# Three early weight conversions placed in later steps of an attention pipeline

## The chip, the cores and the metric

The kernel runs on one core of one Trainium2 chip. The metric is the device time of one execution in microseconds (us). Three executions of the kernel before took 723.31, 723.62 and 725.47 us; the median is 723.62 us.

## The reference

Causal attention with a decay bias, then two feed-forward stages, all in float32. Cut to what matters:

```python
scores = scale * q @ k.T                          # 4 batches, 8 heads, 576 positions, head size 64
cum = cumsum(max(s, 0))
scores = where(causal, -1e9, scores + minimum(-(cum[:, None] - cum[None, :]), 0))
x = softmax(scores) @ v                           # heads joined: 2304 tokens x 512
h = ((x @ w1) * (x @ w2)) @ w3 @ w_out            # w1, w2: 512 x 1024
e = h2 * softmax(h2), h2 = h @ w_in; out = layernorm(e) * g_ln @ w_out2
```

The weights arrive as float64, so the kernel has to turn their bits into float32 itself.

## The kernel before

Attention walks over 32 heads in 36 steps (the loop at line 555). Step `st` computes the scores and the softmax numerators of one head and transposes the probabilities of the head two steps earlier. The first eight heads (batch 0) take steps 0 to 7. Steps 8 and 9 have no scores: they only transpose heads 6 and 7 and multiply by V. From step 10 on, heads 8 to 31 run with the product units of the first feed-forward layer (`ab_unit`, matmuls at line 312, from the table `NF`) between them. The first eight heads use plain float32 matmuls (line 178); later heads use a split into a high and a low word (lines 186 and 187), and each of those splits is made by ACT (line 167, recorded as L94), a DMA (line 168) and one subtraction on POOL (line 169, recorded as L99 on POOL). POOL's first two subtractions, for heads 8 and 9, stand in the steps of heads 6 and 7.

What one head costs on each engine. PE: scores (L178), 13 transposes (L256), and after every second head a pass over V (`av`, L284). DVE: five pieces of row maximum and masking, read from PSUM (L195), a reciprocal (L227, L228), part of the normalisation (L237), and three of six evictions of transposes (L96). ACT: five exponentials (L199), two normalisations (L235), the other three evictions (L94).

A weight conversion (`w_in_job`'s and `wab_job`'s helper `to_f32` at line 345, then `split_w`) takes a staged block of 128 x 512 float64 words and writes a high word and a low word. It is six instructions: ACT scales (L349), DVE shifts (L355) and joins twice (L356, L360), ACT copies the high word (L94, W<-stage), DVE subtracts for the low word (L99, W<-stage,W). All DVE operands lie in SBUF. The block comes by a DMA of 512 KB (L394) into one of two staging buffers; the next load into a buffer waits for the L99 that read it last.

`pump(n)` at line 402 emits n conversions. Its table `PUMP` says how many each step emits, behind the first maximum and exponential of the step's head (`behind`). Sixteen blocks belong to the first layer; three of them are converted before step 10, whose first units need them.

```python
    PUMP = {3: 1, 5: 1, 6: 1, 10: 2, 11: 2, 12: 2, 13: 2, 14: 2, 15: 2, 16: 1}
...
        if st > 1:
            pump(PUMP.get(st, 0))
```

The program's text is not the order on the engines: a scheduler with a model of its own orders each engine's instructions, and the engines then run in that order and wait on semaphores. So a moved conversion can land well away from the step that names it.

Of the kernel before, what the change touches and what calls it, by code (L numbers as in the profile page):

```python
# [26 lines left out]
def tile_attention_moe(  # L27
# [374 lines left out]
    def pump(n):  # L402
        for _ in range(n):
            load_jobs()
            if loaded:
                raw, conv = loaded.pop(0)

                with ExitStack() as order:
                    for ins in behind:
                        order.enter_context(tc.issue_after(ins))  # L410
                    conv(raw)
        load_jobs()
# [135 lines left out]
    steps += [(h if h < NH else None, h - 2 if h >= H + 2 else None) for h in range(H, NH + 2)]  # L548
    NF = {10: 3, 11: 0, 12: 3, 13: 0, 14: 3, 15: 2, 16: 2, 17: 0, 18: 1, 19: 1, 20: 1, 21: 2, 22: 2, 23: 2, 24: 2, 25: 2, 26: 2, 27: 2, 28: 2, 29: 2, 30: 2, 31: 2, 32: 2, 33: 2, 34: 3, 35: 3}
    PD, FS = 10, 0.5  # L550
    PUMP = {3: 1, 5: 1, 6: 1, 10: 2, 11: 2, 12: 2, 13: 2, 14: 2, 15: 2, 16: 1}
    PUMP.update((i, 1 if i < 30 else 2) for i in range(22, 34))
    fill = []
    late = []
    for st, (h, ph) in enumerate(steps):
# [18 lines left out]
        if st > 1:  # L574
            pump(PUMP.get(st, 0))
        if h is not None:
# [461 lines left out]
```

## Time and profile before

| | |
|---|---|
| median of three executions | 723.62 us |
| the profiled execution, its own time | 724.28 us |
| its span, first to last instruction | 722.2 us |
| busy share of PE, DVE, ACT, POOL | 98%, 71%, 65%, 13% |
| mean granted clock of TensorE | 0.998 |
| chain that ended last, by engine | PE 76%, DVE 12%, DMA 4%, ACT 4% |

The profiled execution took 0.66 us more than the median. Its span is 2.1 us shorter than its time; the rest lies before the first and after the last instruction. A busy share over the whole span says little about the first 60 us, where the shares differ from stretch to stretch. "Idle before, releaser" in a row of the timeline is how long the engine stood still ahead of that row and what ended it.

### The profile page before, as it was taken

The page shows a single profiled execution, that of the slowest core. Times are in us where ns is not written, and L with a number is a line of the kernel's source. Part 1 is how long each engine was busy: PE and PEld are TensorE (multiplying, and loading weights), DVE is VectorE, ACT ScalarE, POOL GpSimd, SP SyncE. Part 2 cuts the span into 40 slices and gives each one's busy share as a digit, 9 for nine tenths or more (in the row PEclk, how much of TensorE's full clock was granted, in tenths as well). Part 3 has the DMA queues.
Part 4 walks back from the last instruction along what each step waited for, and adds up shares of the span by engine and source line. Part 5 has one row for each costly group of instructions (what it writes and reads, how often), then busy time and mean ns, then how long its engine had stood idle before and what let it go on. Part 6 is the DMA issues. An engine that isn't in the chain of part 4 may idle for free.

```text
span 722.2 us, 12948 instructions
## 1 busy us (share of the span) xinstructions
PE 706.0 (98%) x4642; PEld 630.9 (87%) x4642; DVE 509.3 (71%) x1252; ACT 467.8 (65%) x978; POOL 94.1 (13%) x88
## 2 busy tenths in 40 slices
PE   9989898999999999999999999999999999999998
PEld 6669888889999999999998889988888988888887
DVE  7997989997878888722787985656747366563751
ACT  7997878798866777822544665656647465564742
POOL 2051322143221221000000000001000000000000
PEclk9999999999999999999999999999999999999999
DMA  4654645454476665514565964242334142303211
GB/s 118 191 138 123 175 154 162 154 147 123 138 231 187 193 183 178 183 63 150 181 209 171 331 207 113 66 110 68 82 87 103 44 131 74 89 13 76 59 45 44
DMA packets 79972, 95.53 MB, mean 132 GB/s; under 512 B 41434, under 2 KB 52954, under 8 KB 79908
## 3 DMA queue, kind: packets, MB, share of 16 engines
q1 hardware_dynamic: 79908, 94.71, 45.2%
q8 instruction: 36, 0.59, 0.3%
q14 instruction: 28, 0.23, 0.1%
HBM read 59.04 MB, written 20.17 MB: 110 GB/s over the span
## 4 chain that ended last, share of the span: by engine, by line
PE 76%; DVE 12%; DMA 4%; ACT 4%; issue 2%; POOL 0%; DVEq 0%; ACTq 0%
PE a L312 12%; PE o L854 12%; PE b L312 12%; PE x L720 11%; PE m L637 6%; PE av L284 4%; PE tr L256 4%; PE hX L752 4%; PE hZ L752 3%; DMA turned<-half 3%; DVE P L195 2%; PE sc L186 2%; PE sc L187 2%; ACT P L199 1%; DMA stage<-in_w_dram 1%
## 5 line engine op out<-in xcount | busy, mean ns | idle before, releaser
L199 ACT ACTIVATE P<-P,STAT 128x576 f32<-128x576 f32 (+4 forms) x160 | 88.2, 553 | 18.7 <-DVE STAT L195 18.1
L99 POOL TENSOR_TENSOR QK<-qk,QK 64x1152 fp32r<-64x1152 f32 x24 | 66.6, 2776 | 169.4 <-ACT QK L94 169.3
L720 PE MATMUL x<-gh,ML 128*128 128x256 f32 x288 | 80.3, 279 | 0.0
L720 PE MATMUL x<-gl,MH 128*128 128x256 f32 x288 | 80.1, 279 | 0.0
L720 PE MATMUL x<-gh,MH 128*128 128x256 f32 x288 | 80.0, 279 | 0.0
L312 PE MATMUL a<-xT0h,W 128*128 128x288 f32 x256 | 58.6, 303 | 3.6 <-ACT PT L94 3.3
L312 PE MATMUL b<-xT0h,W 128*128 128x288 f32 x256 | 57.5, 298 | 1.9 <-DVE g_sb L332 1.7
L854 PE MATMUL o<-OH,lh 128*128 128x512 f32 (+1 forms) x152 | 57.7, 379 | 0.2 <-DVE ll L99 0.2
L816 DVE COPY lt<-turned 128x2048 uint16<-128x2048 uint16 x16 | 21.5, 1344 | 51.1 <-DMA turned<-half 51.1
L854 PE MATMUL o<-OL,lh 128*128 128x512 f32 (+1 forms) x152 | 57.5, 378 | 0.0
L854 PE MATMUL o<-OH,ll 128*128 128x512 f32 (+1 forms) x152 | 57.5, 378 | 0.0
L256 PE MATMUL tr<-ident,P 128*128 128x128 f32 x416 | 54.2, 274 | 3.1 <-DVE PT L96 1.0
L312 PE MATMUL a<-xT1h,W 128*128 128x288 f32 x256 | 57.2, 298 | 0.0
L312 PE MATMUL b<-xT1h,W 128*128 128x288 f32 x256 | 56.5, 294 | 0.0
L720 PEld LDWEIGHTS x<-gl,MH 128*128 128x128 f32 x288 | 54.1, 188 | 1.3
L720 PEld LDWEIGHTS x<-gh,MH 128*128 128x128 f32 x288 | 54.1, 188 | 1.0
L720 PEld LDWEIGHTS x<-gh,ML 128*128 128x128 f32 x288 | 54.1, 188 | 0.8
L96 DVE COPY PT<-tr 64x192 f32<-64x192 f32 (+2 forms) x96 | 40.4, 432 | 17.8 <-PE tr L256 17.8
L349 ACT ACTIVATE stage<-stage 128x512 f32<-128x512 f32 x56 | 37.0, 679 | 24.2 <-DMA stage<-in_w_dram 22.0
L256 PEld LDWEIGHTS tr<-ident,P 128*128 128x128 f32 x416 | 47.1, 141 | 5.8 <-DVE PT L96 1.4
L332 DVE TENSOR_TENSOR g_sb<-b,a_sb 128x288 f32<-128x288 f32 x64 | 28.7, 449 | 30.0 <-PE b L312 20.0
L324 ACT ACTIVATE a_sb<-a 128x288 f32<-128x288 f32 x64 | 25.5, 401 | 36.3 <-PE a L312 36.2
(192 smaller groups left out, 1988.0 us busy)
## 6 DMA issues: line engine op xcount, KB each, us to landing
stage<-in_w_dram SPq DMA_DIRECT2D x32, 512.0 KB
g_scr<-g_sb SPq DMA_DIRECT2D x32, 288.0 KB
stage<-in_wo_dram SPq DMA_DIRECT2D x16, 512.0 KB
qk<-in_qk_dram SPq DMA_DIRECT2D x24, 288.0 KB
QK<-QK SPq DMA_DIRECT2D x24, 288.0 KB
gl<-g_scr SPq DMA_DIRECT2D x24, 256.0 KB
wf<-wf_scr SPq DMA_DIRECT2D x22, 256.0 KB
out_dram<-o SPq DMA_DIRECT2D x17, 256.0 KB
```

Source lines behind the costliest of these rows:

```text
L96: eng.tensor_copy(out=dst, in_=src)
L99: last_lo[0] = eng.tensor_tensor(out=dst, in0=src, in1=hi_.bitcast(F32), op=ALU.subtract).ins
L199: ex = nc.scalar.activation(out=dst, in_=dst, func=AF.Exp, bias=st[0:rows, ti:ti + 1], scale=-1.0, accum_out=st[0:rows, 5 + ti:6 + ti],)
L256: last_tr[0] = nc.tensor.transpose(ps[:, 128 * n:128 * n + 128], pt[:, o:o + 128], ident)
L284: nc.tensor.matmul(st["ps"][64 * e:64 * e + 64, 448 + c0:448 + c1], vr[:, j, e], PT[(2 * p + e) % 4][:, o + c0:o + c1], **kw,)
L312: nc.tensor.matmul(ps, w_[:, c, fs], x_[:, c, sl], start=(c == 0 and w_ is WH and x_ is XH), stop=(c == KC - 1 and w_ is WL),)
L332: ab_last[1] = nc.vector.tensor_tensor(out=g[:, sl], in0=ps, in1=st["a"], op=ALU.mult).ins
L349: nc.scalar.activation(out=high.bitcast(F32), in_=high.bitcast(F32), func=AF.Copy, scale=2.0 ** -112)
L637: nc.tensor.matmul(ps, w_[:, k % 4], o_[:, k], start=(k == 0 and w_ is H3 and o_ is WOH), stop=(k == KF - 1 and w_ is L3),)
L720: last = nc.tensor.matmul(ps[:, a], w_[:, k, m * 128:m * 128 + 128], g_[:, k % 2], start=(k == 0 and w_ is MH and g_ is GH), stop=(k == KF ...
L752: last_h[0] = nc.tensor.matmul(ps, x_[:, k], w_[:, k], start=first and k == 0 and x_ is XH and w_ is WH, stop=k == 1 and x_ is XL, skip_gr ...
L854: last = nc.tensor.matmul(ps, l_[:, k], w_[:, k, c0:c1], start=(k == 0 and l_ is LH and w_ is OH), stop=(k == KF - 1 and l_ is LL),)
```

## The change

One table entry per conversion moves: the first early conversion from step 3 to step 6, the second from step 5 to step 8, the third from step 6 to step 9.

```diff
-    PUMP = {3: 1, 5: 1, 6: 1, 10: 2, 11: 2, 12: 2, 13: 2, 14: 2, 15: 2, 16: 1}
+    PUMP = {6: 1, 8: 1, 9: 1, 10: 2, 11: 2, 12: 2, 13: 2, 14: 2, 15: 2, 16: 1}
```

What the scheduler makes of it, at three places. In the rows, P and STAT_116 to STAT_119 belong to heads whose number leaves 0 to 3 when divided by 4, and PT_112 to PT_115 are the transposed probabilities of the same heads; here they are heads 4 to 7. W_122 and W_123 are the high and low words of w1, W_124 and W_125 those of w2. QK_657 and QK_641 are one tile, that of head 9, under two numbers.

DVE around the last maxima of head 7 (STAT_119), before:

```order
L237 TENSOR_SCALAR P<-P,STAT_118 128x192
L96 COPY PT_112<-tr 64x3x64
L237 TENSOR_SCALAR P<-P,STAT_118 64x64
L195 ISA P,STAT_119<-sc,wmask 128x448
L195 ISA STAT_119 128x1
L195 ISA P,STAT_119<-sc,wmask 64x64
L195 ISA STAT_119 64x1
L99 TENSOR_TENSOR W_123<-stage,W_122 128x4x128
L195 ISA P,STAT_119<-sc,wmask 128x320
L195 ISA STAT_119 128x1
L195 ISA P,STAT_119<-sc,wmask 128x192
L195 ISA STAT_119 128x1
```

and with the change, from the end of the same maxima on:

```order
L99 TENSOR_TENSOR W_125<-stage,W_124 128x4x128
L195 ISA P,STAT_119<-sc,wmask 128x320
L195 ISA STAT_119 128x1
L195 ISA P,STAT_119<-sc,wmask 128x192
L195 ISA STAT_119 128x1
L96 COPY PT_113<-tr 128x512
L237 TENSOR_SCALAR P<-P,STAT_118 64x64
L355 TENSOR_SCALAR stage<-stage 128x512
L96 COPY PT_113<-tr 64x3x64
L96 COPY PT_113<-tr 128x128
L96 COPY PT_114<-tr 128x512
L356 SCALAR_TENSOR_TENSOR stage<-stage 128x512
```

Before, all three conversions end ahead of head 7's last maximum, two of them far ahead. With the change two whole conversions stand between head 6's first maximum and head 7's last one, and the third conversion's L355 and L356 stand among the evictions that follow.

ACT between head 7's exponentials, with the change (before, there is no conversion from the row of QK_657 to the end of head 7's normalisation):

```order
L199 ACTIVATE P,STAT_119<-P,STAT_119 128x448
L199 ACTIVATE P,STAT_119<-P,STAT_119 64x64
L235 ACTIVATE P<-P,STAT_118 128x576
L235 ACTIVATE P<-P,STAT_118 128x448
L94 ACTIVATE QK_641<-qk_587 64x2x576
L94 ACTIVATE PT_113<-tr 128x384
L349 ACTIVATE stage<-stage 128x512
L94 ACTIVATE PT_113<-tr 128x256
L199 ACTIVATE P,STAT_119<-P,STAT_119 128x320
L199 ACTIVATE P,STAT_119<-P,STAT_119 128x192
```

The third conversion's L349 now stands ahead of head 7's last two exponentials; its high word (L94, W_122) stands ahead of head 7's L235, a few rows further on.

SP's queue with the change, where the loads of the third, fourth and fifth block now stand (before, the third and fourth stood ahead of head 8's rows of cum_scr, and the fifth where the third stands now):

```order
L140 DMA qk_743<-in_qk_dram 64x1152
L394 DMA stage<-in_w_dram 128x1024
L158 DMA QK_641<-cum_scr 2x576
L159 DMA QK_641<-cum_scr 2x576
L394 DMA stage<-in_w_dram 128x1024
L168 DMA QK_641<-QK_641 64x2x576
L140 DMA qk_897<-in_qk_dram 64x1152
L394 DMA stage<-in_w_dram 128x1024
L148 DMA VT_120<-in_vm_dram 128x512
```

The loads moved behind the conversions that free their buffers. POOL's order is unchanged throughout, and from the first scores of head 8 on (QK_596 before, QK_580 now) every engine's order is the same as before.

## Rows read from the trace of the kernel before

**Rows 1.** Busy time of one stretch: us, then busy us and count of PE, PEld, DVE, ACT, POOL; PEclk, DMA, GB/s.

```profile
46.00:52.00 6.00, 3.86 (x26) 2.68 (x25) 5.43 (x18) 5.95 (x17) 3.56 (x5) 1.00 0.49 144
```

**Rows 2.** Timeline of PE: start us, us, engine, line, operation, tile, count, idle before.

```profile
35.48 0.44 PE L256 MATMUL tr<-ident,P 128*128 128x128 f32 x2
35.75 1.14 PE L178 MATMUL sc<-QKN 128*128 128x288 f32 x4
...
45.68 1.13 PE L178 MATMUL sc<-QKN 128*128 128x320 f32 x4 [0.27 <-DVE PT L96]
47.78 1.97 PE L256 MATMUL tr<-ident,P 128*128 128x128 f32 x13 [0.97 <-DVE STAT L195]
...
51.69 1.21 PE L256 MATMUL tr<-ident,P 128*128 128x128 f32 x9 [0.79 <-DVE PT L96]
...
57.51 0.47 PE L186 MATMUL sc<-QK 128*128 128x448 f32 x1
```

**Rows 3.** Timeline of DVE from head 6's first maximum to head 7's last one.

```profile
37.58 0.74 DVE L195 CUSTOM_DVE_ANT_0 P<-sc,lmask 128x576 f32<-128x576 f32 x1
...
38.25 0.42 DVE L355 TENSOR_SCALAR stage<-stage 128x512 uint32<-128x512 uint32 x1
...
40.47 0.68 DVE L96 COPY PT<-tr 128x512 f32<-128x512 f32 x1
41.07 0.71 DVE L356 SCALAR_TENSOR_TENSOR stage<-stage 128x512 uint32<-128x512 uint32 x1
...
42.43 2.42 DVE L360 SCALAR_TENSOR_TENSOR stage<-stage 128x512 uint32<-128x512 uint32 x1
44.75 0.60 DVE L237 TENSOR_SCALAR P<-P,STAT 128x320 f32<-128x320 f32 x2
...
45.35 0.28 DVE L96 COPY PT<-tr 128x128 f32<-128x128 f32 x1
...
46.45 0.34 DVE L96 COPY PT<-tr 64x192 f32<-64x192 f32 x1
46.72 0.24 DVE L237 TENSOR_SCALAR P<-P,STAT 64x64 f32<-64x64 f32 x1
...
47.56 0.68 DVE L99 TENSOR_TENSOR W<-stage,W 128x512 fp32r<-128x512 f32 x1
...
48.85 0.75 DVE L99 TENSOR_TENSOR xT0l<-av,xT0h 128x576 fp32r<-128x576 f32 x1
```

**Rows 4.** Timeline of POOL: three of the 24 subtractions of the query and key split.

```profile
41.57 2.71 POOL L99 TENSOR_TENSOR QK<-qk,QK 64x1152 fp32r<-64x1152 f32 x1
...
93.52 3.91 POOL L99 TENSOR_TENSOR QK<-qk,QK 64x1152 fp32r<-64x1152 f32 x1 [10.30 <-ACT QK L94]
109.13 2.68 POOL L99 TENSOR_TENSOR QK<-qk,QK 64x1152 fp32r<-64x1152 f32 x1 [11.69 <-ACT QK L94]
```

**Rows 5.** Timeline of DVE beside the last two of those.

```profile
94.22 0.68 DVE L99 TENSOR_TENSOR W<-stage,W 128x512 fp32r<-128x512 f32 x1
...
109.64 2.46 DVE L355 TENSOR_SCALAR stage<-stage 128x512 uint32<-128x512 uint32 x1
```

**Rows 6.** Timeline of ACT in the step of head 7.

```profile
45.53 0.65 ACT L94 ACTIVATE W<-stage 128x512 fp32r<-128x512 f32 x1
...
46.88 1.33 ACT L235 ACTIVATE P<-P,STAT 128x576 f32<-128x576 f32 x2
...
48.27 0.66 ACT L199 ACTIVATE P<-P,STAT 128x448 f32<-128x448 f32 x1
...
49.38 1.16 ACT L94 ACTIVATE QK<-qk 64x1152 fp32r<-64x1152 f32 x1
```

**Rows 7.** The chain of waits: start us, us, what; the wait for a staged block.

```profile
69.05 3.49 DMA stage<-in_w_dram
```

**Rows 8.** PE's longest wait of the first 200 us, and the stretch behind it (columns as in rows 1).

```profile
119.26 0.58 PE L312 MATMUL a<-xT0h,W 128*128 128x288 f32 x1 [3.34 <-ACT PT L94]
...
120.00:122.00 2.00, 2.00 (x10) 2.00 (x9) 2.00 (x8) 0.87 (x2) 0.00 (x0) 0.50 0.42 149
```

## The prediction

> **What bounds the kernel now.** I read the timeline first, because the change ends where head 8 begins: from its first scores on, every engine's order is unchanged, so whatever it gains or loses is the shift of that one PE row, at 57.51 us [rows 2]. Past it nothing waits on a clock of its own; a shift there is carried to the end one for one.
>
> The busy table by stretch comes next: from 46 to 52 us PE is busy only 3.86 of 6.00 us [rows 1]. In its timeline no row between 24 and 45 us names a wait, and then three long ones do: 0.27, 0.97 and 0.79 us, all of them ended by DVE [rows 2]. From 51.69 us to head 8's scores PE runs unbroken for 5.82 us (9 transposes, a pass over V, 13 transposes). So up to 45 us PE is the limit and conversions lie beside it; from 45 to 52 us DVE is. No row of DVE between 32 and 50 us names a wait.
>
> The last view is DVE against POOL. L360 takes 2.42 us at 42.43, while POOL's subtraction runs from 41.57 to 44.28; its successor starts at 44.75 [rows 3, 4]. L356 just ahead needs 0.71. Unhindered, successors start 0.07 to 0.08 us before a row ends, so L360 costs 0.60 and was held for 1.72.
>
> **The change, part by part.** It removes and adds no work; it moves three conversions.
>
> *Taken out of the time before 36 us.* Up to there DVE sheds all eight rows of the first two conversions and ACT all four of theirs. I cost this at nothing: PE is without a wait, and covers them. What remains is a small gain at head 6's first maximum. DVE reached it at 37.58, after PE had finished the scores of the row at 35.75 [rows 2, 3]. Now DVE is there in time and PE sets it. In the new order the two transposes of 35.48 stand behind those scores, so they take from 35.48 to about 36.5, and DVE starts at 36.6: 0.98 us earlier.
>
> *Put in, up to head 7's last maximum.* Before, that stretch of DVE takes 48.85 - 37.58 = 11.27 us with one conversion in it [rows 3]. The new order has two: 0.34 (L355) + 0.63 (L356) + 0.60 (L360) + 0.61 (L99) = 2.18 us more. It also gains the low word of xT0 (0.67) and one 128 x 128 eviction (0.20) and loses two 64-wide normalisations (0.16 each): +0.55. The hold by POOL's first subtraction stays at 1.72, since some conversion row is there whenever it starts. The stretch is 14.0 us and ends at 36.6 + 14.0 = 50.6, against 48.85. **Term A: +1.75.**
>
> *From there to PE's nine transposes.* Before: 51.69 - 48.85 = 2.84. After: eviction of 512 (0.60), L237 (0.16), the third L355 (0.34), evictions of 64 x 192 and 128 (0.27 + 0.20) [rows 3], and 0.1 to PE: 1.67. **Term B: -1.17.** A and B alone put head 8's scores at 58.1.
>
> *The second hold.* POOL's next subtraction (head 9) starts when ACT has its high words. Behind head 7's second maximum ACT has two exponentials (1.11, the spacing to the next row), L235 (1.23 of the 1.33), and the high words (1.16): 3.5 us [rows 6]. DVE, from the same maximum, has 0.09 + 0.67 + 0.20 + 0.53 + 0.61 + 0.40 + 0.28 + 0.60 + 0.16 = 3.54 us to the third L355 (spans of rows 3 less their overlap; 0.09, 0.40 and 0.28 are the spacings of the reciprocal and the last two maxima). That is a tie. If POOL is first, L355 waits out nearly all of 2.65 us, and the evictions that PE needs wait behind it: +2.6. If DVE is first, the evictions pass (they read PSUM) and L356 is held; head 7's normalisation then sets the end. From POOL's start: 2.65 + L356 0.63 + eviction 0.27 + L360 0.60 + ACT's high word 0.57 [rows 6] + L235 1.23 + 13 transposes 1.57 + 0.2 for hand-overs = 7.7. POOL starts at 50.6 + 1.1 = 51.7, so scores at 59.4, which is 1.3 over 58.1. I take the middle, **term C: +2.0**, as nothing in the rows breaks the tie; the ends are 0 (no conversion row meets it) and 2.6.
>
> That POOL holds L355 so long is a row: 2.46 us at 109.64, beside the subtraction of 109.13 [rows 4, 5]. The other order of arrival is one too: at 93.52 POOL took 3.91 us for what is else 2.7, while DVE's L99 at 94.22 kept its 0.68 [rows 4, 5].
>
> [...]
>
> *DMA.* SP's loads move behind the conversions that free the buffers. The first L99 now ends at about 47.1 (50.6 less the 3.5 us of rows behind it), so the third block lands 3.49 us later [rows 7], at 50.6; ACT reaches its L349 at about 51.7. Slack 1.1 us: no cost. Without it head 7's last two exponentials would stand behind a DMA. SP's own rows of head 9 and 10 now stand behind loads that wait for DVE; their scores start only after 68 us, so I cost that at nothing. V's load behind the fifth block serves heads 8 and 9, equally late.
>
> Sum: 1.75 - 1.17 + 2.0 = **+2.6 us**. The profiled 724.28 would become 726.9; it stood 0.66 above the median of 723.62, so I predict **726.2 us**.
>
> **Rivals.**
>
> *Only the first hold bites (A and B alone).* +0.6 us: 724.2. It needs POOL's second subtraction to run while DVE is in evictions or maxima, as in the step of head 6 where maxima passed beside it. Against it: two SBUF rows of the third conversion stand in just that place.
>
> *Faster: DVE is relieved.* ACT and DVE shed twelve rows before 36 us; if that carries over, DVE meets head 7's maxima early and PE's waits at 45.68, 47.78 and 51.69 vanish, 2.03 us in all: 721.6. If only the holds miss DVE, A falls to 0 and the change gives 1.1: 722.5. It decides if head 7's last maximum ends before 48 us. Against it: PE covers all that is shed, and two conversions come back into the stretch where DVE has no gap.
>
> [...]
>
> *The change doesn't do what it says.* Partly so: by name two conversions move to steps without scores, but on DVE and ACT their rows stand ahead of head 7's last maxima and exponentials. That is in the sum already.
>
> **How the numbers follow.** About 0.3%, 2.2 us, is what a measurement here can tell from no change. Forecast (+1.2 to +3.7): 0.50, of which 0.36 lie above 2.2 us. Worse: 0.12. Only the first hold (0 to +1.2): 0.26. Faster: 0.12, of which 0.08 is by more than 2.2 us, as several waits must vanish at once. So faster 0.08, same 0.14 + 0.26 + 0.04 = 0.44, slower 0.48. The range goes from 722.5, which takes in both holds missing DVE, to 728.2, just short of the clock case in full; somewhat over 0.1 is left out.
>
> **What would show it.** Right: head 7's last maximum ends near 50.6 us in the timeline of DVE; one of the conversion rows between 41 and 46 us takes over 2 us, and L355 or L356 between 51 and 55 us as well; head 8's scores start near 60 us; PE's waits from 45 us on grow from 2 to over 4 us; the span grows as much as that row shifts. Wrong: head 7's last maximum before 49 us, or conversion rows all at their usual 0.4 to 0.7, or head 8's scores late and the span not.

## The result, and the profile after

| | before | after |
|---|---|---|
| median, lowest and highest of 6 runs each (us) | 724.06 (723.04 to 725.47) | 730.65 (728.69 to 732.63) |
| ratio, 95% interval | | 1.0091 (1.0075 to 1.0108) |
| profiled execution, its span (us) | 724.28, 722.2 | 728.69, 726.8 |
| mean granted clock | 0.998 | 0.993 |
| forecast of the median (range) | | 726.2 (722.5 to 728.2) |

The change costs 0.9%. The sign was forecast, the size was not: the median lies 2.45 us above the range. The profiled execution of the changed kernel is the fastest of its six. Of all executions below, one is left out of its ratio: 992.7 us in third_only, at a mean granted clock of 0.656.

The rows below are PE's in the timeline of the changed kernel (columns as in [rows 2]).

```profile
46.78 1.13 PE L178 MATMUL sc<-QKN 128*128 128x320 f32 x4 [1.38 <-ACT PT L94]
...
51.77 1.69 PE L256 MATMUL tr<-ident,P 128*128 128x128 f32 x7 [1.98 <-DVE STAT L195]
55.38 2.18 PE L256 MATMUL tr<-ident,P 128*128 128x128 f32 x9 [1.91 <-DVE PT L96]
57.48 3.79 PE L284 MATMUL av<-PT,VT 128*64 128x64 f32 x24
61.21 1.64 PE L256 MATMUL tr<-ident,P 128*128 128x128 f32 x13
62.80 0.44 PE L186 MATMUL sc<-QK 128*128 128x448 f32 x1
...
124.53 0.58 PE L312 MATMUL a<-xT0h,W 128*128 128x288 f32 x1 [3.34 <-ACT PT L94]
```

Head 8's first scores moved from 57.51 [rows 2] to 62.80, by 5.29 us. The row that stood at 119.26 [rows 8] stands at 124.53, 5.27 later, with the same stop ahead of it. The spans differ by 4.6: some 0.7 comes back after 128 us, 0.31 of it at one wait of PE that shrinks from 0.53 to 0.22 us (at 142.82 before, at 147.73 after). So the place is right: everything is lost before head 8. Two more things are in these rows. The stops of [rows 2] (0.27, 0.97, 0.79) have become 1.38, 1.98 and 1.91, and the first of them is now ended by ACT. And the nine transposes take 2.18 instead of 1.21 us.

The busy table of the same stretch (columns as in [rows 1]) tells why:

```profile
50.00:52.00 2.00, 0.23 (x2) 0.23 (x3) 2.00 (x7) 1.95 (x4) 0.48 (x2) 1.00 0.19 70
52.00:54.00 2.00, 1.41 (x7) 0.77 (x5) 2.00 (x2) 1.98 (x6) 2.00 (x1) 0.61 0.92 314
54.00:56.00 2.00, 0.62 (x3) 0.63 (x4) 2.00 (x6) 0.51 (x3) 0.47 (x1) 0.50 0.54 123
56.00:58.00 2.00, 2.00 (x12) 1.66 (x12) 0.93 (x3) 0.84 (x3) 0.00 (x0) 0.50 0.37 120
58.00:60.00 2.00, 2.00 (x8) 0.94 (x6) 1.96 (x7) 1.68 (x4) 0.00 (x0) 0.68 0.00 0
```

The granted clock falls from 1.00 to 0.50 and stays there until about 59 us. Before, it was 1.00 through this whole stretch:

```profile
52.00:54.00 2.00, 2.00 (x17) 1.44 (x16) 1.87 (x4) 1.56 (x6) 1.25 (x1) 1.00 0.65 134
54.00:56.00 2.00, 2.00 (x20) 1.64 (x16) 0.76 (x4) 1.30 (x4) 0.00 (x0) 1.00 0.57 147
56.00:58.00 2.00, 2.00 (x17) 1.75 (x15) 1.52 (x3) 1.20 (x3) 0.00 (x0) 1.00 0.56 152
```

With the change DVE has no gap from 50 to 56 us, and these are its rows that matter:

```profile
36.74 0.76 DVE L195 CUSTOM_DVE_ANT_0 P<-sc,lmask 128x576 f32<-128x576 f32 x1 [0.92 <-PE sc L178]
...
40.85 0.73 DVE L355 TENSOR_SCALAR stage<-stage 128x512 uint32<-128x512 uint32 x1
41.47 0.67 DVE L237 TENSOR_SCALAR P<-P,STAT 64x64 f32<-64x64 f32 x1
...
44.05 2.10 DVE L356 SCALAR_TENSOR_TENSOR stage<-stage 128x512 uint32<-128x512 uint32 x1 [0.38 <-ACT stage L349]
...
49.23 1.21 DVE L237 TENSOR_SCALAR P<-P,STAT 128x320 f32<-128x320 f32 x2
...
51.64 0.68 DVE L96 COPY PT<-tr 128x512 f32<-128x512 f32 x1
52.25 2.27 DVE L237 TENSOR_SCALAR P<-P,STAT 64x64 f32<-64x64 f32 x1
```

Beside them, POOL (columns as in [rows 4]):

```profile
42.80 2.79 POOL L99 TENSOR_TENSOR QK<-qk,QK 64x1152 fp32r<-64x1152 f32 x1
48.02 0.58 POOL L483 MEMSET QK<- 64x576 f32 x1 [2.43 <-issue]
...
49.68 0.64 POOL L486 MEMSET QK<- 2x576 f32 x1
51.84 2.63 POOL L99 TENSOR_TENSOR QK<-qk,QK 64x1152 fp32r<-64x1152 f32 x1 [1.52 <-ACT QK L94]
```

The two 2 us rows of DVE, L356 and the 64 x 64 L237, lie under POOL's two subtractions; usual are 0.7 and 0.24 us [rows 3]. The pair of L237 at 49.23 lies under the last two of four memsets and takes 1.21 instead of 0.60. The chain of waits carries the first two as pieces of their own:

```profile
44.05 2.10 DVE stage L356
52.32 2.20 DVE P L237
```

### The profile page after: what moved, and what is told of

The parts are those of the page before. It is cut to its first block, busy times and chain, and to the rows that moved or that the text cites. A ratio compares the mean times of both kernels' runs of the same rounds, so it can differ in the third digit from the quotient of the medians.

```text
span 726.8 us, 12951 instructions
## 1 busy us (share of the span) xinstructions
PE 707.8 (97%) x4642; PEld 631.9 (87%) x4642; DVE 510.7 (70%) x1252; ACT 469.1 (65%) x978; POOL 94.4 (13%) x88
## 4 chain that ended last, share of the span: by engine, by line
PE 79%; DVE 10%; DMA 5%; ACT 3%; issue 2%; POOL 0%; DVEq 0%; ACTq 0%
PE a L312 13%; PE b L312 12%; PE o L854 12%; PE x L720 11%; PE m L637 6%; PE av L284 5%; PE tr L256 5%; PE hX L752 4%; PE hZ L752 3%; DMA turned<-half 3%; PE sc L178 2%; PE sc L187 2%; PE sc L186 2%; DVE P L195 2%; PE hW L752 1%
## 5 line engine op out<-in xcount | busy, mean ns | idle before, releaser
L256 PE MATMUL tr<-ident,P 128*128 128x128 f32 x416 | 55.7, 279 | 4.8 <-DVE PT L96 2.1
L96 DVE COPY PT<-tr 128x512 f32<-128x512 f32 (+2 forms) x96 | 40.3, 431 | 19.3 <-PE tr L256 18.7
L349 ACT ACTIVATE stage<-stage 128x512 f32<-128x512 f32 x56 | 36.9, 677 | 23.7 <-DMA stage<-in_w_dram 21.2
L195 DVE CUSTOM_DVE_ANT_0 P<-sc,wmask 128x448 f32<-128x448 f32 (+3 forms) x128 | 47.2, 412 | 2.7 <-PE sc L187 1.7
```

What stands on the lines that cost most here:

```text
L96: eng.tensor_copy(out=dst, in_=src)
L195: mx = nc.vector.tensor_tensor_reduce(out=dst, in0=ps_in, in1=msk, scale=-SCALE, scalar=BIG, op0=ALU.add, op1=ALU.min, accum_out=st[0:rows ...
L256: last_tr[0] = nc.tensor.transpose(ps[:, 128 * n:128 * n + 128], pt[:, o:o + 128], ident)
L349: nc.scalar.activation(out=high.bitcast(F32), in_=high.bitcast(F32), func=AF.Copy, scale=2.0 ** -112)
```

## The experiments

The theory after these rows: POOL's rows hold DVE's (a hold is a row of DVE that lasts longer while a row of POOL runs beside it), PE runs dry, and its clock falls. In most runs below each engine's order is fixed, instruction by instruction, to that of the kernel named, and only the edit differs; "waits for" is a real wait on a semaphore. Lines of an edit are rows of an engine's order. Medians are read by their ratio to the kernel before, run on the same chip.

**The changed kernel again** (after_again).

> The changed kernel once more, for a second profile. Holds theory (POOL's rows hold DVE's, PE runs dry, its clock falls): the same rows again, L356 over 2 us near 44 us, the 64 x 64 L237 over 2 us near 52 us, granted clock at 0.5 from about 53 to 59 us, head 8's first scores at 62.8 us or later; time 730.6 us. Where this profile is slower than the first one (728.7 us), the difference should lie in a longer stretch at the lower clock, here or at 120 us. Rival (a disturbance of the one profiled execution): L356 and L237 at their usual 0.6 and 0.2 us and head 8's scores near 58 us.

730.0 us, 1.0085 (1.0065 to 1.0104). The same holds (the second profile has the same rows), and a lower clock for longer: 0.82, 0.50, 0.50, 0.50 and 0.97 in the five stretches from 52 to 62 us. One row shows it, the pass over V:

```profile
57.17 4.37 PE L284 MATMUL av<-PT,VT 128*64 128x64 f32 x24
```

From the transposes that waited for head 7's last maximum to head 8's scores it took 63.07 - 51.40 = 11.67 us, against 62.80 - 51.77 = 11.03 in the first profile. So these two profiles differ by how long the clock stays down.

**POOL's second subtraction out of the way** (hold2).

```diff
 POOL
-L99 QK<-qk (head 9)
+L99 QK<-qk (head 9), waits for DVE L237 P 64x64 of head 7
```

> Every engine's order is that of the changed kernel; POOL's subtraction for head 9 waits for the last normalisation of head 7 (DVE, near 60 us). Holds theory: the 64 x 64 L237 near 52 us falls from 2.27 to about 0.2 us, head 7's last maximum stays at 51.6 us, head 8's first scores come at 51.6 + 1.7 + 5.8 = 59.1 us, the granted clock stays at 1.00 from 52 to 60 us; the time is 3 to 4 us below the changed kernel's, about 727 us. Work theory (the conversions' own time on DVE is the loss, POOL only stands beside it): head 8's scores stay later than 62 us and the time at 730 us.

726.72 us, 1.0034 (1.0017 to 1.0051): 3.3 us below the changed kernel. DVE first, then PE:

```profile
52.27 0.24 DVE L237 TENSOR_SCALAR P<-P,STAT 64x64 f32<-64x64 f32 x1
```

```profile
51.80 3.74 PE L256 MATMUL tr<-ident,P 128*128 128x128 f32 x16 [1.99 <-DVE STAT L195]
55.47 2.94 PE L284 MATMUL av<-PT,VT 128*64 128x64 f32 x24
...
59.94 0.44 PE L186 MATMUL sc<-QK 128*128 128x448 f32 x1
```

The hold is real, and the scores came 2.86 us earlier. But they missed 59.1: the sixteen transposes took 3.74 us, as the clock fell here too, behind a stop of 1.99 us:

```profile
52.00:54.00 2.00, 2.00 (x10) 1.47 (x10) 1.75 (x6) 1.98 (x6) 0.00 (x0) 0.53 0.80 286
54.00:56.00 2.00, 2.00 (x13) 1.49 (x13) 1.27 (x4) 1.27 (x6) 0.00 (x0) 0.61 0.51 123
```

**PE kept busy in its stops, holds left in place** (fill with 7 unused matmuls of 128 x 512, fill22 with 4).

```diff
 PE
-L284 av 64x64
 L256 tr (head 5), six of nine
+L291 av<-wmask,ident 128x512 x2
 L256 tr x7
+L291 av<-wmask,ident 128x512 x2
 L256 tr x9
+L284 av 64x64
```

They write where the pass over V starts its sums anew; its first 64-wide matmul moves behind the transposes. The trace records each of them as two. The 7 of fill are 3 and 4.

> The order of the changed kernel, with 7 matmuls more on PE that compute nothing used (128 x 512, 3 in the gap before 51.8 us, 4 in the gap before 55.4 us; two 64-wide matmuls of the pass over V are taken from between transposes to its start). Clock theory (the idle PE is what lowered the granted clock, and the lower clock cost 1.6 us): the clock stays near 1.00 from 52 to 60 us, the nine transposes take 1.2 instead of 2.18 us, the pass over V 2.9 instead of 3.8, head 8's scores come at about 61.2 us, and the time is some 1.5 us below the changed kernel's, 729 us, with more work. Rival (the clock falls for another reason, or what PE loses by it is hidden): clock and scores as before, time 730.6 us or up to 1 us more.

> The changed kernel with 4 unused matmuls instead of 7 in PE's two stops (2 and 2), as in the run with 7 those of the second stop ran about 1 us past the eviction that PE waits for. Clock theory: clock at 1.00 or nearly from 52 to 60 us, nine transposes 1.2 us, head 8's scores at 55.4 + 5.8 = 61.2 us or up to 0.5 earlier, time 726 to 727 us, 3 to 4 us below the changed kernel with the same holds in place. Rival (the gain of the run with 7 came from the moved 64-wide matmuls or from elsewhere): no difference to that run, 727.3 us, or a fall of the clock all the same.

fill: 727.31 us (expected: 729), 1.0044 (1.0027 to 1.0061); its clock was 1.00 from 46 to 64 us. fill22: 726.9 us, 1.0020 (1.0003 to 1.0038), with 1.00 from 48 to 62. PE in fill22, and two lines of its busy table:

```profile
52.88 1.88 PE L291 MATMUL av<-wmask,ident 128*128 128x512 f32 x4
55.35 1.20 PE L256 MATMUL tr<-ident,P 128*128 128x128 f32 x9 [0.60 <-DVE PT L96]
...
61.05 0.44 PE L186 MATMUL sc<-QK 128*128 128x448 f32 x1
```

```profile
54.00:56.00 2.00, 1.40 (x8) 0.65 (x7) 2.00 (x6) 0.48 (x3) 0.46 (x1) 1.00 0.68 147
56.00:58.00 2.00, 2.00 (x18) 1.03 (x17) 1.86 (x7) 1.46 (x4) 0.00 (x0) 1.00 0.32 108
```

Nine transposes start when they did (55.38) and take 1.20 instead of 2.18 us; head 8's scores come 1.75 us earlier. More work made the kernel faster, so the lower clock is a price of its own: 1.75 us in the profile, and by the ratios some 3 us (fill) to 5 us (fill22) in the medians, each uncertain by more than 1 us.

**Both edits together** (hold2_fill: hold2, and 2 unused matmuls in the first stop).

> The run with POOL's second subtraction moved, and 2 matmuls more on PE that compute nothing used, in its stop ahead of head 7's last maximum (49.8 to 51.8 us). That run's clock fell to 0.53 and 0.61 from 52 to 56 us although PE was busy from 51.8 us on. Clock theory (that stop alone brings the fall): the clock stays at 1.00 from 52 to 56 us, head 8's scores come 0.8 to 0.9 us earlier (59.1 instead of 59.94 us), the time is about 0.8 us lower or more, 725.5 us. Rival (the fall comes from what PE did after the stop, or from elsewhere): the fall stays, and the time at 726.7 us.

725.73 us, 1.0015 (1.0006 to 1.0024); the clock is 1.00 from 44 to 60 us, and head 8's scores come as expected (59.1):

```profile
59.03 0.44 PE L186 MATMUL sc<-QK 128*128 128x448 f32 x1
```

With that one stop filled, the fall of hold2 is gone.

**POOL's first subtraction out of the way as well** (nohold, then nohold_b).

```diff
 POOL
-L99 QK<-qk (head 8)
 L483 to L486 MEMSET QK (head 9)
+L99 QK<-qk (head 8), waits for DVE L237 P 64x64 of head 6
 L99 QK<-qk (head 9), waits for DVE L237 P 64x64 of head 7
 SP
-L140 qk<-in_qk (head 10)
 L394 stage, L158, L159, L394 stage
+L140 qk<-in_qk (head 10)
 DVE
-L355, L356 (third conversion) among the evictions
+L355, L356 (third conversion) behind them
```

nohold has the waits and the DVE part alone, with POOL's memsets behind its subtraction. "The run before" in its expectation is hold2.

> As the run before, and POOL's subtraction for head 8 and its next four memsets wait for the last normalisation of head 6, with the first two DVE rows of the third conversion behind the evictions that PE waits for. Holds theory: L356 near 44 us takes 0.7 instead of 2.10 us, the two L237 near 49 us 0.6 instead of 1.21; head 7's last maximum ends at about 49.6 us, head 8's first scores come at 49.6 + 1.7 + 5.8 = 57.1 us, as early as in the kernel before (57.5) although both conversions still stand there; time about 724 us. Work theory: head 8's scores at 60 us or later, time 728 us or more.

> As the run in which both subtractions wait, but without what stopped it (ACT stood 7.14 us for the third block, whose load stood on SP behind head 10's words, which waited for POOL): head 10's words are loaded after the two blocks, and POOL makes its second four memsets ahead of the subtraction for head 8. Holds theory: L356 0.7 us, the two L237 near 49 us 1.2 us again (memsets beside them), head 7's last maximum at 51.6 - 1.4 = 50.2 us, head 8's scores at 50.2 + 1.7 + 5.8 = 57.7 us; the granted clock falls little or not, since PE's stop ahead of head 7's last maximum shrinks from 2.0 to 0.6 us; time 724 to 725 us, no slower than the kernel before. Work theory: not below the run with the second subtraction alone moved (726.7 us).

nohold: 734.55 us, 1.0154 (1.0121 to 1.0187). Locally DVE did as expected (L356 0.69, the L237 pair 0.60, head 7's last maximum 2.0 us closer to its first one), but ACT stood still:

```profile
58.99 0.65 ACT L349 ACTIVATE stage<-stage 128x512 f32<-128x512 f32 x1 [7.14 <-DMA stage<-in_w_dram]
```

SP's load of head 10's words waits until POOL has read the buffer, and the third block's load is queued behind it. nohold_b moves it: 726.46 us, 1.0029 (1.0016 to 1.0042). Its DVE, POOL and PE rows:

```profile
44.06 0.69 DVE L356 SCALAR_TENSOR_TENSOR stage<-stage 128x512 uint32<-128x512 uint32 x1 [0.37 <-ACT stage L349]
...
47.86 0.60 DVE L237 TENSOR_SCALAR P<-P,STAT 128x320 f32<-128x320 f32 x2
48.38 0.68 DVE L99 TENSOR_TENSOR W<-stage,W 128x512 fp32r<-128x512 f32 x1
...
49.67 0.68 DVE L96 COPY PT<-tr 128x512 f32<-128x512 f32 x1
```

```profile
48.16 0.82 POOL L483 MEMSET QK<- 64x576 f32 x1 [5.42 <-ACT P L199]
```

```profile
58.83 0.44 PE L186 MATMUL sc<-QK 128*128 128x448 f32 x1
```

Head 7's last maximum now ends at 49.67, 2 us earlier than in the changed kernel, and yet the scores gain only 0.2 us on hold2_fill. PE waits for ACT instead (0.38 us on an eviction, 0.42 on L235), and for a DVE eviction that waited for ACT (0.73). I expected 57.7 and 724 to 725 us, and the time alone is what the work theory said: another bound stood right behind the one taken away.

**ACT's conversion rows behind the evictions, and DVE's behind head 7's normalisation** (nohold_act, then nohold_sp). The two move together; no run parts them.

```diff
 ACT
-L349 stage (third conversion)
 L94 PT x1, L199 x2, L94 PT x4
+L349 stage (third conversion)
-L94 W<-stage
 L235 x2, L94 xT0h
+L94 W<-stage
 DVE
-L355, L356, L360, L99 W (third conversion)
 L227, L96, L228, L237 x3 (head 7)
+L355, L356, L360 (third conversion)
 L96, L99 xT0l, L96
+L99 W (third conversion)
 POOL
-L99 QK<-qk (head 9), waits for DVE L237 P 64x64 of head 7
+L99 QK<-qk (head 9), waits for that L99 W
```

nohold_sp also puts the fifth block's L394 and V's load on SP ahead of head 11's words.

> The run in which neither subtraction meets a conversion, and the third conversion's rows stand behind head 7's: ACT's L349 behind the evictions of head 5 and 6 (it stood ahead of them at 51.44 us), ACT's high word W behind the eviction of the pass over V, DVE's four rows behind head 7's normalisation. There head 8's scores were still at 58.83 us, 1.3 behind the kernel before, with PE waiting 0.73, 0.38 and 0.42 us on evictions and L235. Theory now (holds, and behind them ACT's conversion rows ahead of evictions that PE waits for): those waits shrink to 0.3 us or less, head 8's scores at 57.5 to 57.9 us, as in the kernel before although both conversions stand there; time 724.5 to 725.5 us. Rival (the rest is the DVE work ahead of head 7's last maximum, which isn't touched here): scores stay at 58.8, time at 726.5 us.

> The run with the conversion rows behind head 7's, with one thing more: SP loads the fifth block and V ahead of the words of head 11, which wait for POOL's second subtraction. In that run head 8's scores came at 57.60 us, as in the kernel before, but the block that stood on SP behind those words landed at 69 us, ACT waited 4.56 and DVE 7.00 us for it, and PE stopped for 2.96 and 1.48 us. Theory (POOL's holds and ACT's conversion rows ahead of evictions are the whole loss of the change, and the rest of that run's 730.0 us was the late block): scores at 57.6 us, no stop of PE over 1 us between 62 and 80 us, time 724 to 725.5 us. Rival (two conversions in that stretch cost time in whatever order, later if not there): time at 726.5 us or more with the block there in time.

nohold_act: head 8's scores at 57.60 us, as in the kernel before, but 730.01 us, 1.0076 (1.0056 to 1.0096): a block loaded late stopped PE for 2.96 and 1.48 us near 70 us. nohold_sp: 724.7 us, 1.0011 (0.9991 to 1.0031), with the scores here:

```profile
57.77 0.44 PE L186 MATMUL sc<-QK 128*128 128x448 f32 x1
```

Both conversions still stand ahead of head 7's last maximum, and the time can't be told from that of the kernel before. So their work alone doesn't cost; it cost together with POOL's holds and with the third conversion's rows where the scheduler had put them.

**One part of the change alone** (third_only).

```diff
-    PUMP = {6: 1, 8: 1, 9: 1, 10: 2, 11: 2, 12: 2, 13: 2, 14: 2, 15: 2, 16: 1}
+    PUMP = {3: 1, 5: 1, 9: 1, 10: 2, 11: 2, 12: 2, 13: 2, 14: 2, 15: 2, 16: 1}
```

> One part of the change alone: the first two conversions stay in the steps of heads 3 and 5, only the third moves from head 6's step to the second step without scores. Holds theory: one conversion in the stretch that DVE bounds, as before, and one hold by POOL's first subtraction, now on L355 instead of L360; head 7's last maximum within 0.5 us of 48.85 us, head 8's scores within 1 us of 57.51 us, time 723 to 725 us. Rival (it is the third conversion's move that costs, by its load and its ACT row ahead of head 7's exponentials): most of the loss is there, 727 us or more.

724.98 us, 1.0004 (0.9990 to 1.0018), scores at 57.80 us. One conversion in the stretch costs nothing measurable, in either of the two places tried. Head 7's last maximum ended at 49.78, 0.93 us behind the kernel before and outside the 0.5 that I gave. The hold fell on another row than the L355 that I named, DVE's smallest, of five columns:

```profile
42.73 2.24 DVE L227 TENSOR_SCALAR STAT<-STAT 128x5 f32<-128x5 f32 x1 [0.30 <-ACT P L199]
```

PE had its longest stop of this stretch here, longer than that of hold2, and the clock stayed at 1.00 from 44 to 60 us:

```profile
47.84 1.10 PE L178 MATMUL sc<-QKN 128*128 128x320 f32 x4 [2.42 <-DVE STAT L195]
```

**The hold of the kernel before taken away** (before_nohold).

```diff
 POOL
-L99 QK<-qk (head 8)
+L99 QK<-qk (head 8), waits for DVE L237 P 64x64 of head 6
 DVE
-L99 W (third conversion) between head 7's maxima
+L99 W (third conversion) behind the evictions of heads 5 and 6
```

> The order of the kernel before; POOL's subtraction for head 8 waits for the last normalisation of head 6, and the third conversion's L99 stands behind the evictions of head 5 and 6 instead of between head 7's maxima. Holds theory: L360 takes 0.6 instead of 2.42 us at 42.4 us, head 7's last maximum comes 1.7 + 0.6 = 2.3 us earlier on DVE (46.5 us) until PE's own rows set it, PE's waits at 45.68, 47.78 and 51.69 us (2.03 us in all) shrink; head 8's scores 1 to 2 us earlier (55.5 to 56.5 us) and the time 722 to 723 us. Rival (PE's order sets that stretch, DVE's hold lies beside it): scores at 57.5 us, time 724.2 us.

724.45 us, 0.9997 (0.9979 to 1.0015). L360 fell from 2.42 to 0.71, and head 7's last maximum came 1.8 us earlier (47.06 against 48.85). Head 8's scores stand where they did. DVE's two rows, then PE:

```profile
42.44 0.71 DVE L360 SCALAR_TENSOR_TENSOR stage<-stage 128x512 uint32<-128x512 uint32 x1
...
51.63 0.29 DVE L96 COPY PT<-tr 128x128 f32<-128x128 f32 x1 [1.08 <-ACT PT L94]
```

```profile
57.51 0.47 PE L186 MATMUL sc<-QK 128*128 128x448 f32 x1
```

The rival was right. In the kernel before, the hold cost nothing measurable: without it DVE waits 1.08 us for ACT at the eviction that PE waits for, and the end is the same.

**A hold that does cost, in the kernel before** (pool120, pool120_act). PE's 3.34 us stop [rows 8] has the same anatomy: POOL subtracts from 114.30 us, L360 at 114.67 takes 2.83 us, and ACT's high word waits 0.89 us for it ahead of PE's evictions.

```diff
 POOL
-L99 QK<-qk (the row at 114.30 us)
+L99 QK<-qk (the row at 114.30 us), waits for DVE L237 P 64x64 (the row at 118.28 us)
```

pool120_act has this as well:

```diff
 ACT
-L94 W<-stage, L349 stage
 L94 PT x3
+L94 W<-stage, L349 stage
 DVE
-L355 stage
 L237, L96 x2, L332, L195 lmask
+L355 stage
```

> The kernel before, unchanged up to 110 us; the one POOL subtraction at 114.30 us waits for the last normalisation that DVE has at 118.28 us. In the kernel before it holds L360 (2.83 instead of 0.68 us at 114.67), ACT's high word waits 0.89 us for that row ahead of PE's evictions, and PE stops for 3.34 us, after which its clock is at 0.50 for over 3 us. Holds theory: L360 0.7 us, PE resumes at 118.2 instead of 119.26 us, a stop of 2.3 us; where no fall of the clock follows, another 1.3 us: time 722 to 723 us. Rival (as with the hold at 42 us in this kernel, the hold lies beside ACT's own rows): PE resumes at 119 us, time 724.4 us.

> The run before this one, and ACT makes its three evictions of the transposes ahead of the two conversion rows that stand before them (high word and L349), with DVE's L355 three rows later. Holds and order theory: the first eviction follows the exponential at 116.6 us, PE resumes at about 117.3 us, a stop of 1.3 us, without a fall of the clock; time 721 to 722 us, faster than both kernels. Rival (another wait, DVE's evictions or the block's load, takes the place): PE resumes at 118 us or later, time above 723 us.

pool120: 721.0 us, 0.9950 (0.9932 to 0.9968). DVE and PE:

```profile
114.48 0.72 DVE L360 SCALAR_TENSOR_TENSOR stage<-stage 128x512 uint32<-128x512 uint32 x1
```

```profile
117.36 0.37 PE L312 MATMUL a<-xT0h,W 128*128 128x288 f32 x1 [1.63 <-DVE PT L96]
```

The stop is 1.63 us, shorter than the 2.3 expected, and the clock stays at 1.00 from 112 to 130 us. pool120_act: 720.28 us, 0.9957 (0.9942 to 0.9972); the stop is 0.99 us, but a new wait of 0.46 us follows 3 us later. The two can't be told apart. One added wait makes the kernel before 3 to 4 us faster, and these are the fastest of all that ran.

## Why the prediction was wrong in size

All values are of the profiled executions, up to head 8's scores.

| step | forecast | measured | by |
|---|---|---|---|
| head 6's first maximum starts | 36.6 | 36.74 | row above |
| term A, to head 7's last maximum | +1.75 | +2.79 | 51.64 against 48.85 |
| term B, from there on without a hold | -1.17 | -1.28 | hold2_fill: 59.03 - 51.65 = 7.38, before 8.66 |
| term C, the second hold | +2.0 | +2.02 | fill22 against hold2_fill: 61.05 - 59.03 |
| PE's clock | 0 | +1.75 | after against fill22: 62.80 - 61.05 |
| sum | +2.6 | +5.28 | 62.80 - 57.51 = 5.29 |

*What bounds the kernel.* The reading that DVE bounds PE from 45 to 52 us was half of it. before_nohold and nohold_b relieve DVE by about 2 us and gain nothing or 0.2: ACT's evictions come next, at nearly the same time. That also takes the ground from the rival "Faster".

*Term A.* Its work items were right, and the first hold nearly: L356 has 2.02 us to the next row instead of 0.60, a hold of 1.42, not 1.72. The term is short by 1.04 us all the same, because only POOL's subtraction was counted as a holder. Memsets hold DVE's `tensor_scalar` rows too: 0.61 us on the L237 pair at 49.23, which nohold gives back by moving those memsets (0.60 again). The first four memsets added 0.31 us to L355 and 0.43 to the L237 behind it; these rows overlap, and no run took those memsets away. A wait of 0.38 us on ACT comes on top.

*Terms B and C.* Right in size. For C that is luck: the tie that it stood for went POOL's way, for which the forecast was +2.6, not the middle; and so early that the subtraction met the L237 ahead of L355 (2.27 instead of 0.24 us). The evictions wait behind it just the same. Without any hold the prediction's terms come to 1.75 - 1.72 - 1.17 = -1.1 us, and that did not come: nohold_sp is at +0.26 (57.77 against 57.51), as ACT is next there. That evictions and maxima pass beside a subtraction, as the prediction has it, is in the rows: in the changed kernel the 128 x 512 eviction at 43.00, under POOL's row of 42.80, took 0.67 us, against 0.68 at 51.64, and in the kernel before the maximum at 41.79, under that of 41.57 [rows 4], took 0.72, against 0.74 at 37.58 [rows 3]. Why these pass, no run shows. One reading behind C isn't shown: POOL's row at 93.52 [rows 4], taken for DVE coming first, starts 0.10 us ahead of the first of the two DVE rows beside it (L356 at 93.62, 0.68 us). The rows show that POOL paid there, not who came first.

*The clock.* This is the step that failed: the sum granted PE full speed, a term of 0 where 1.75 us was measured in the profile. The chance of 0.12 for "Worse" stands for a fall of the clock behind a long stop, and its price of 1.5 us was my estimate from [rows 8]: 1 us lost in 2 us at a granted clock of 0.50, and 0.5 us for the two ends. With term C at 2.6 that makes 728.3, the clock case that the range ends just short of. The price was about right for the profile (nine transposes took 2.18 us at 0.50 and 1.20 at 1.00), the chance was not: I had tied it to one stop nearly as long as the 3.34 us of [rows 8]. What came were stops of 1.38, 1.98 and 1.91 us, and in hold2 the clock fell behind one of 1.99, ahead of which PE had been busy for 2.85 of 4 us. The forecast already had PE standing still for over 4 us in pieces from 45 us on. The length of a stop alone doesn't tell, though: behind the 2.42 us of third_only the clock stayed at 1.00.

*From the profile to the median.* The forecast took the profiled execution to lie 0.66 us above the median, as before. In the changed kernel it lies 1.96 below. These 2.62 us are more than half of what the median is off (730.65 - 726.2 = 4.45), and no profile of a slower execution parts them. In part they are the draw of one execution: 35 of the kernel before, run beside nohold_b, reach from 721.93 to 728.04 us. The clock has a share, argued and not shown: the three of those 35 with a mean clock of 1.000 took 721.93 to 722.80, unused matmuls that keep the clock up gain more in the medians than the 1.75 us of the profile, and after_again's profile lost 0.64 us more behind the same stops. But four of the changed kernel's six executions have the same mean clock, 0.993, at 728.69 to 730.77 us.

*DMA.* Right for the change itself: L349 found its block there, and no row of the stretch waits for a load. nohold and nohold_act show what a late block costs: there loads stood on SP behind a row that waits for POOL.

## What to carry to other kernels

When work is moved into a stretch, count what every row of POOL there does to DVE, memsets included (here 0.61 us on one pair of rows), and then look which engine is next behind DVE: the gain of a relief ends there. Where PE will stand still several times in a row, as here, put the clock into the sum, at its price (here 1.75 us) times a chance, and don't wait for one long stop: the fall came behind 1.99 us in one run and not behind 2.42 in another. To move a POOL row, follow the DMA queue that waits for it first; done at the right place, one wait was worth 0.5%.

## What the runs showed that I had not expected

The same stop can cost 1.3 us more or not. Ahead of the row at 119.26 [rows 8] a stop of 3.3 us or more is in every kernel here but the two made to shorten it. In eleven profiles the clock fell behind it: in ten of them to a mean of 0.50 to 0.57 in the lowest stretch of 2 us, and in nohold the unit of matmuls behind it took 2.94 us. In the two below it stayed at 1.00 (hold2 first, then nohold_sp):

```profile
121.86 0.37 PE L312 MATMUL a<-xT0h,W 128*128 128x288 f32 x1 [3.30 <-ACT PT L94]
```

```profile
120.65 0.37 PE L312 MATMUL a<-xT0h,W 128*128 128x288 f32 x1 [3.34 <-ACT PT L94]
```

The unit of matmuls behind it took 1.66 us in hold2 (121.86 to 123.52) against 3.00 before (119.26 to 122.26). What parts the two outcomes of one stop, no run here shows.

Which DVE rows a memset held went by their kind here. Under memsets, `tensor_scalar` rows waited (L237 1.21 instead of 0.60), while the low word, which reads two SBUF operands, kept its 0.68 us beside the memset of 48.16 in nohold_b; that memset, begun under an L237, took 0.82 instead of 0.58. Why the two kinds differ, no run here shows. And size is no shelter: a `tensor_scalar` on five columns took 2.24 us in third_only, against 0.16 at 45.28 in the kernel before. Ahead of it POOL had paid, too: its subtraction, begun 0.07 us behind an L355, took 3.38 us instead of 2.7, while that L355 and the pair of L237 behind it kept their 0.45 and 0.60.
